# The last matrix product of a fused attention and two feed-forward layers: all twelve features by seven products, product number outermost

## The chip, the cores and the metric

The kernel runs on one core of one Trainium2 chip. The metric is the device time of one execution in microseconds (us). The engines are named as in the profile: PE (TensorE, matmuls), PEld (its weight loads), DVE (VectorE), ACT (ScalarE), POOL (GpSimd) and SP (SyncE, which issues the transfers).

## The reference, cut to what matters

```
def reference(...):                       # float32 in and out
    attn = causal attention of q, k, v    # 2 x 12 heads x 448 positions x 64
    x = attn.transpose(0, 2, 1, 3).reshape(896, 768)
    h = x @ w_in;  x = (h - tanh(h)) @ w_out          # 768 -> 2048 -> 768
    a = x @ w_a;   b = x @ w_b                        # 768 -> 1536 each
    return (a * b) @ w_o                              # 1536 -> 768
```

The change concerns the last line: the product of g = a * b (896 tokens, 1536 features) with w_o. In the kernel everything lies transposed: features on partitions in 12 blocks of 128 (f), tokens along the columns in two batches of 448 (B0, B1), outputs in 6 blocks of 128 (dm). The weights come as 64-bit floating point numbers, which the kernel makes into float32 on the chip.

## The kernel before, in words

**Precision.** Every float32 product is made of three matmuls of rounded operands: high by high, high by low and low by high (lines 275 to 284). So every operand, weight or feature, is made into two halves: ACT copies it into the high half, DVE subtracts that from the operand and writes the low half (`halve`, lines 600 to 602, for features; lines 244 and 253 for weights).

**Seven products.** Where two blocks of inputs, two of outputs and two batches stand together as 2 x 2 matrices, the kernel makes the four outputs with seven products in place of eight (a Strassen form after Winograd). The products have the numbers 1 to 7. Products 1 and 2 give one output, and 6, 3 and 5, 7, 4 are added up in the banks on the way to the others. The price is sums and differences of weights and of features, on DVE. One product over three blocks of inputs is 9 matmuls of 448 columns.

**Weights.** A weight tile (768 inputs by 128 outputs) is loaded in two transfers by SP's queue into one of three `raw` buffers (line 170), ACT casts its upper bits (line 179, `top`), DVE joins them with the lower ones to a float32 tile `t` (line 193, four buffers), and the halves `wh`, `wl` go into one of five pairs of buffers (WB). A list, `plan`, says in which order the weight halves are needed. `advance` (line 260) moves each of these steps one on, and every product calls it. `in_turn` (line 112) writes the plan of a stage in which the products of neighbouring outputs interleave.

**The stage of w_a and w_b.** Twelve units of two output blocks, w_a and w_b by turns, each by seven products over three pairs of inputs (`turn`, line 724): 63 matmuls a unit. `times` (line 710) multiplies the outcome of a w_b unit with that of the w_a unit before it, into the float32 features `g32`: one tile for each feature block, with both batches abreast.

**The last product.** Features 0 to 5 go by seven products with the pairs (0,3), (1,4), (2,5), and features 6 to 11 directly. For each of three pairs of outputs the kernel makes products 1, 5, 2, 3, 6, 7 and 4 (`seven`, 9 matmuls each), and between them four direct products of six features (`rest`, 18 matmuls each), which are added to the same banks. The terms of the features are made ahead: `early_terms` during the last unit of the stage before in the code, `late_terms` behind it. `kept` (line 856) copies a bank with ACT, `add` (line 696) adds a bank to a copy with DVE, `put` (line 861) issues the output's transfer.

**What sets the order.** The attention is written in an order by hand. After it, a scheduler places the instructions of each engine when the program is built, by its own estimates of their times; each engine then runs its list in that order, and waits where an instruction's inputs or buffers are not ready.

Of the kernel before, what the change touches and what calls it, by code (L numbers as in the profile page):

```python
# [9 lines left out]
F32 = mybir.dt.float32  # L10
F32R = mybir.dt.float32r
BF16 = mybir.dt.bfloat16
I32 = mybir.dt.int32
# [38 lines left out]
def attention_moe_moe2(ctx, tc, q, k, v, w_in, w_out, w_a, w_b, w_o, out):  # L52
# [22 lines left out]
    WB = 5  # L75
    scale = 1.0 / float(D) ** 0.5
# [62 lines left out]
    u0 = len(units)  # L139
    for f in range(0, NF2, 2):  # L140
        for w in (w_a, w_b):
            pair(w, f)
    in_turn(u0, True)
    for dm in range(0, KD, 2):
        pair(w_o, dm)
        u = len(units) - 1
        plan.extend((u, m) for m in (1, 5, 2, 3))
        whole(block(w_o, slice(DM, 2 * DM), dm))
        plan.extend((u, m) for m in (6, 7))
        whole(block(w_o, slice(DM, 2 * DM), dm + 1))  # L150
        plan.append((u, 4))
    last_use = {}
    for j, (i, m) in enumerate(plan):
        for x in (i,) if m is None else (units[i], units[i] + 1):
# [3 lines left out]
    thirds, summed = {}, set()  # L158
# [23 lines left out]
    def bits():  # L182

        i = at["bits"]
        while at["t"] in last_use and last_use[at["t"]] < at["halve"]:
# [6 lines left out]
        ts[i] = tp.tile([128, KD, 128], I32, tag="t", name="t")[:, 0:nk]  # L192
# [3 lines left out]
        at["bits"] += 1  # L196

    def source(j):

        i, m = plan[j]  # L200
        if m is None:
            return ts[i].bitcast(F32)
        if m == 7:
# [16 lines left out]

    def split_high():
# [4 lines left out]
        full = m is None  # L226
        if not full and j > at["halve"]:
            return
        if (i if full else units[i] + int(m not in (1, 2))) >= at["bits"]:
            return  # L230
# [6 lines left out]
        if m in (3, 5, 6, 7):  # L237
            combine(i, m)
# [471 lines left out]
    def times(u, q, x, on_chip):  # L710

        f, b = u // 2 * 2 + q // 2, q % 2
        if u % 2 == 0:
            if not on_chip:
                e = etile()
                nc.scalar.copy(out=e, in_=x)
                x = e
            left[q] = x
            return
        if f not in g32:  # L720
            g32[f] = g_full[0].tile([128, NT], F32, tag=("gwh", "gwl")[f // NK if f < KD else f % 2], name="g32")
        nc.vector.tensor_tensor(out=g32[f][:, BATCHES[b]], in0=x, in1=left.pop(q), op=ALU.mult)
# [72 lines left out]
    last, wide = [{} for _ in range(NK)], {}  # L795

    def early_terms(kk):

        g1, g2 = g32[kk], g32[kk + NK]
        t = [partp.tile([128, NT], F32R, tag="part", name="gpart") for _ in range(2)]  # L800
        last[kk][1], last[kk][5] = [[x[:, cs] for x in t] for cs in BATCHES]
        halve(*last[kk][1], g1[:, B0])
        minus(g1[:, B0], g1[:, B1], g1[:, B0])
        halve(*last[kk][5], g1[:, B0])
        minus(g1[:, B1], g2[:, B1], g1[:, B1])

    def roomy(f):

        if f == NF2 - 1:
            return small(2)  # L810
        pool, tags = (xp, ("xh", "xl")) if f < KD + NK else (xtra, ("th", "tl"))
        t = [pool.tile([128, NT], F32R, tag=x, name=x) for x in tags]
        return [[x[:, cs] for x in t] for cs in BATCHES]

    def split_wide(cs):

        for f in range(KD, NF2):
            if f not in wide:
                wide[f] = roomy(f)
            halve(*wide[f][cs.start // S], g32[f][:, cs])  # L820

    def late_terms():

        for kk in range(NK):
            t = [xp.tile([128, NT], F32R, tag=x, name=x) for x in ("xh", "xl")]
            last[kk][2], last[kk][3] = [[x[:, cs] for x in t] for cs in BATCHES]
        for m, cs in ((2, B0), (3, B1)):
            for kk in range(NK):
                halve(*last[kk][m], g32[kk + NK][:, cs])
        for kk in range(NK):  # L830
            g2 = g32[kk + NK]
            minus(g2[:, B1], g2[:, B1], g32[kk][:, B0])
            minus(g2[:, B0], g2[:, B0], g2[:, B1])
        split_wide(B0)
        for kk in range(NK):
            last[kk][7], = small()
            halve(*last[kk][7], g32[kk][:, B1])
        for m, cs in ((6, B1), (4, B0)):
            for kk in range(NK):
                t = g_full[0].tile([128, NT], F32R, tag="gwh", name="gwh")  # L840
                last[kk][m] = [t[:, x] for x in BATCHES]
                halve(*last[kk][m], g32[kk + NK][:, cs])
            if m == 6:
                split_wide(B1)

    def seven(o, m, go_on=False, done=1):

        wh, wl = next_weights()
        product(o, [((wh[:, kk], wl[:, kk]), last[kk][m]) for kk in range(NK)], go_on=go_on)
        at["done"] += done  # L850
        advance()

    def rest(w, o, cs, go_on=True):
        product(o, [((w[0][:, f - KD], w[1][:, f - KD]), wide[f][cs.start // S]) for f in wide], go_on=go_on)
# [14 lines left out]
    late_terms()  # L869
    for dm in range(0, KD, 2):  # L870
        o1, o5, o2, o3 = [next_bank()[:, :S] for _ in range(4)]
        seven(o1, 1)
        r0 = kept(o1)
        seven(o5, 5)
        r3 = kept(o5)
        seven(o2, 2)
        seven(o5, 3, True)
        w = next_weights()
        rest(w, o2, B0)
        add(r0, o2)  # L880
        put(dm, B0, r0)
        seven(o1, 6, True, 0)
        r1 = kept(o1)
        rest(w, o5, B1)
        add(r1, o5)
        put(dm, B1, r1)
        at["done"] += 3
        advance()
        seven(o1, 7, True)
        add(r3, o1)  # L890
        w = next_weights()
        rest(w, o3, B1, False)
        add(r3, o3)
        put(dm + 1, B1, r3)
        seven(o1, 4, True, 0)
        rest(w, o1, B0)
        put(dm + 1, B0, kept(o1))
        at["done"] += 4
        advance()
        advance()  # L900
# [27 lines left out]
```

## Time and profile before

| | us |
|---|---|
| runs | 558.43, 561.26, 558.07 |
| median | 558.43 |
| the profiled execution | 559.96 |
| its span | 558.2 |
| PE busy | 548.0 |
| DVE busy | 425.1 |
| ACT busy | 331.0 |

The profile shows one execution; its span begins with the first and ends with the last instruction, and 1.8 us of the execution's time lie around it. Busy times are of the whole span, which has stages with different limits: what a change in one stage is worth is read there. Matmuls are pipelined, so one that is busy for 0.37 us can start 0.2 us after the one before it.

### The profile page before, as it was taken

The numbers are of one execution on the slowest core, as the hardware profiler recorded it, in microseconds if no ns is written. First come the engines' busy times: TensorE is split into PE (matmuls) and PEld (weight loads), VectorE is DVE, ScalarE is ACT, GpSimd is POOL, SyncE is SP. The second block draws the span as 40 slices with busy tenths as digits, with TensorE's granted clock in tenths as the row PEclk, the third lists the DMA queues.
The fourth block names the chain that finished last, engine by engine and source line by source line (L and its number), as shares of the span: only waits on it lengthen the run. The fifth ranks groups of instructions, "written<-read, shape, count | busy, mean of one in ns | idle before, by whom it ended". The sixth has DMA issues, their size and how long they took to land.

```text
span 558.2 us, 8730 instructions
## 1 busy us (share of the span) xinstructions
PE 548.0 (98%) x3121; PEld 486.3 (87%) x3121; DVE 425.1 (76%) x876; ACT 331.0 (59%) x706; POOL 65.8 (12%) x88
## 2 busy tenths in 40 slices
PE   8999999998999999999999999999999999999997
PEld 4777788897999899899899889999999999999996
DVE  6897886479988867549879988979788699985311
ACT  6997996457677843238756464665554558754120
POOL 5688672200000000000000000000000000000000
PEclk9999999999999999999999999999999999999999
DMA  8825350067133742313741115335343533432001
GB/s 259 249 83 150 89 147 1 1 189 225 56 115 116 234 129 86 112 57 99 218 136 57 54 60 178 112 106 169 104 132 105 169 100 100 138 109 90 34 33 49
DMA packets 70827, 64.94 MB, mean 116 GB/s; under 512 B 13952, under 2 KB 70784, under 8 KB 70784
## 3 DMA queue, kind: packets, MB, share of 16 engines
q1 hardware_dynamic: 70784, 64.40, 37.0%
q8 instruction: 24, 0.39, 0.3%
q14 instruction: 19, 0.16, 0.1%
HBM read 61.63 MB, written 2.75 MB: 115 GB/s over the span
## 4 chain that ended last, share of the span: by engine, by line
PE 90%; DVE 3%; DMA 3%; ACT 2%; issue 1%; SPq 0%; DVEq 0%; ACTq 0%
PE s L280 37%; PE t L280 20%; PE h L280 13%; PE o L280 8%; PE o L432 4%; PE s L371 4%; PE t L406 3%; ACT p L392 1%; DMA raw<-in_moe_w_out 1%; PE t L451 1%; PE h L406 1%; DVE xsum L637 1%; DVE t L193 1%; DMA v<-in_v 1%; DMA raw<-in_moe_w_in 1%
## 5 line engine op out<-in xcount | busy, mean ns | idle before, releaser
L244 ACT CAST wh<-t 128x384 fp32r<-128x384 f32 (+2 forms) x154 | 81.9, 562 | 86.0 <-PE s L280 37.7
L179 ACT CAST top<-raw 128x768 f16<-128x768 bf16 (+1 forms) x70 | 73.8, 1054 | 44.7 <-DVE t L193 11.8
L253 DVE TENSOR_TENSOR wl<-t,wh 128x384 fp32r<-128x384 f32 (+2 forms) x149 | 87.0, 605 | 17.4 <-ACT wh L244 17.2
L193 DVE SCALAR_TENSOR_TENSOR t<-raw,top 128x768 int32<-128x768 int32 (+1 forms) x70 | 68.8, 985 | 4.0 <-ACT top L179 3.7
L280 PE MATMUL s<-xl,wh 128*128 128x448 f32 x150 | 55.0, 367 | 0.0
L280 PE MATMUL s<-xh,wl 128*128 128x448 f32 x150 | 54.7, 366 | 0.0
L280 PE MATMUL s<-xh,wh 128*128 128x448 f32 x150 | 54.2, 367 | 0.2 <-ACT e L733 0.2
L392 ACT ACTIVATE p<-p,m 112x448 f32<-112x448 f32 (+3 forms) x96 | 49.9, 524 | 5.6 <-DVE m L383 5.3
L697 DVE TENSOR_TENSOR e<-s,e 128x448 f32<-128x448 f32 x33 | 20.4, 620 | 31.8 <-PE s L280 31.5
L383 DVE CUSTOM_DVE_ANT_0 p<-s,mask 112x448 f32<-112x448 f32 (+3 forms) x96 | 37.9, 441 | 7.3 <-PE s L371 6.7
L280 PE MATMUL s<-gwl,wh 128*128 128x384 f32 (+2 forms) x96 | 34.9, 365 | 0.3 <-DVE gwl L558 0.3
L280 PE MATMUL s<-gwh,wl 128*128 128x384 f32 (+2 forms) x96 | 34.9, 365 | 0.0
L280 PE MATMUL s<-gwh,wh 128*128 128x512 f32 (+2 forms) x96 | 34.3, 364 | 0.0
L280 PEld LDWEIGHTS s<-xh,wh 128*128 128x128 f32 x150 | 28.2, 188 | 2.9 <-ACT e L733 0.6
L280 PEld LDWEIGHTS s<-xh,wl 128*128 128x128 f32 x150 | 28.2, 188 | 2.3
L280 PEld LDWEIGHTS s<-xl,wh 128*128 128x128 f32 x150 | 28.2, 188 | 2.3
L406 PE MATMUL t<-ident,p 112*112 112x112 f32 x195 | 27.6, 265 | 0.2 <-POOL qkh L351 0.2
L432 PE MATMUL o<-pt,v 112*64 112x224 f32 (+1 forms) x288 | 26.7, 326 | 0.9 <-DMA v<-in_v 0.9
L414 ACT COPY pt<-t 112x448 f32<-112x448 f32 (+1 forms) x39 | 18.4, 483 | 14.8 <-PE t L406 12.8
L432 PEld LDWEIGHTS o<-pt,v 112*64 112x64 f32 x288 | 19.1, 136 | 8.3 <-issue 1.1
L280 PE MATMUL h<-xh,wh 128*128 128x448 f32 x69 | 25.8, 374 | 0.0
L280 PE MATMUL h<-xh,wl 128*128 128x448 f32 x69 | 25.7, 372 | 0.0
(213 smaller groups left out, 1442.2 us busy)
## 6 DMA issues: line engine op xcount, KB each, us to landing
raw<-in_moe_w_out SPq DMA_DIRECT2D x48, 383.2 KB, 3.8
raw<-in_moe_w_in SPq DMA_DIRECT2D x32, 383.2 KB, 4.2
raw<-in_moe_w_a SPq DMA_DIRECT2D x24, 383.2 KB, 3.9
raw<-in_moe_w_b SPq DMA_DIRECT2D x24, 383.2 KB, 3.7
raw<-in_moe_w_out SPq DMA_DIRECT2D x12, 255.5 KB, 4.3
qk<-in_q SPq DMA_DIRECT2D x12, 224.0 KB, 3.3
qk<-in_k SPq DMA_DIRECT2D x12, 224.0 KB, 4.0
v<-in_v SPq DMA_DIRECT2D x24, 112.0 KB, 3.5
```

The source lines that it names most:

```text
L179: nc.scalar.copy(out=tops[i % len(tops)][:, 0:nk, :, 1], in_=top[:, :, :, 2])
L193: nc.vector.scalar_tensor_tensor(out=ts[i], in0=low[:, :, :, 0], scalar=13, in1=top, op0=ALU.logical_shift_right, op1=ALU.bitwise_or)
L244: nc.scalar.copy(out=halves[j][0], in_=x)
L253: engine.tensor_tensor(out=lo, in0=source(j), in1=hi.bitcast(F32), op=ALU.subtract)
L280: nc.tensor.matmul(o, a, b_, start=j == 0 and not go_on, stop=j == n - 1, skip_group_check=True)
L371: nc.tensor.matmul(sc[i, c][e], a[r, 0, cs], b_[r, 1, :n], start=x == 0, stop=x == len(terms) - 1)
L383: nc.vector.tensor_tensor_reduce(out=p[:, e], in0=s, in1=mask[:QC, S - n:], scale=-scale, scalar=3.0e38, op0=ALU.add, op1=ALU.min, accum_o ...
L392: nc.scalar.activation(out=p[:, e], in_=p[:, e], func=ACTF.Exp, bias=least[i][:, c, e:e + 1], scale=-1.0, accum_out=sums[i][:, c, e:e + 1],)
L406: nc.tensor.transpose(out=pst[:QC, x * QC:(x + 1) * QC], in_=blk, identity=ident[:QC, :QC])
L414: nc.scalar.copy(out=out_, in_=in_)
L432: nc.tensor.matmul(o[64 * e:64 * e + 64, cs], vt[:, k_, e, :], p.rearrange("s c q -> s (c q)"), start=k_ == 0, stop=k_ == 2 * h + 1, skip_ ...
L697: nc.vector.tensor_tensor(out=x, in0=o, in1=x, op=ALU.add)
```

## The change

All twelve features now go by the seven products: feature f is paired with f + 6, so that a product is 6 blocks of inputs, 18 matmuls. `g32` holds two neighbouring features of one batch abreast in a tile of 896 columns, so one instruction of ACT or DVE makes a term, or a half of it, for two features (`term`). The product number is outermost: product 1 for all three pairs of outputs, then 2, and so on in the order LAST; the outputs being added up stay in banks and copies meanwhile. The terms are made in the order of the products, a few ahead (AHEAD). A weight of the last product is a whole tile of 768 inputs, and its sums go over the whole tile (`combine_quad`). The six tiles of the odd output blocks (`of_last` with home "part") are loaded and joined between the tiles of w_a and w_b, from the sixth unit on; the other six keep their place behind them.

```diff
+    AHEAD = (1, 0, 2)
+    FIRST_LAST = 5
...
+    LAST = (1, 2, 5, 3, 6, 7, 4)
+    homes, quads = {}, {}
+    for n in range(KD // 2):
+        quads[u0 + NF2 + n] = {}
+
+    def of_last(n, r, f, home):
+        quads[u0 + NF2 + n][1 + r, 1 + f] = len(tiles)
+        homes[len(tiles)] = home
+        tiles.append(block(w_o, slice(f * DM, (f + 1) * DM), 2 * n + r))
+
     for f in range(0, NF2, 2):
         for w in (w_a, w_b):
             pair(w, f)
+            n = len(units) - 1 - u0 - FIRST_LAST
+            if 0 <= n < KD:
+                of_last(n // 2, 1, n % 2, "part")
     in_turn(u0, True)
-    for dm in range(0, KD, 2):
-        pair(w_o, dm)
-        u = len(units) - 1
-        plan.extend((u, m) for m in (1, 5, 2, 3))
-        whole(block(w_o, slice(DM, 2 * DM), dm))
-        plan.extend((u, m) for m in (6, 7))
-        whole(block(w_o, slice(DM, 2 * DM), dm + 1))
-        plan.append((u, 4))
+    for f in range(2):
+        for n in range(KD // 2):
+            of_last(n, 0, f, "t" if 3 * f + n < 4 else ("th", "tl")[n % 2])
+    units.extend([None] * len(quads))
+    plan.extend((u, m) for m in LAST for u in quads)
...
-        if i >= at["abs"] or i >= at["t"] + TP:
+        home = homes.get(i, "t")
+        held_ = sum(homes.get(x, "t") == "t" for x in range(at["t"], i))
+        if i >= at["abs"] or home == "t" and held_ >= TP or home in ("th", "tl") and not last_turned:
...
+        if home == "t":
+            ts[i] = tp.tile([128, KD, 128], I32, tag="t", name="t")[:, 0:nk]
+        else:
+            t = (partp if home == "part" else xtra).tile([128, NT], I32, tag=home, name="tlast")
+            ts[i] = t[:, 0:KD * 128].rearrange("p (k n) -> p k n", n=128)
...
+        if home == "part" and i in [x[2, 2] for x in quads.values()]:
+            a21, a22 = [ts[i_].bitcast(F32) for x in quads.values() if x.get((2, 2)) == i for i_ in (x[2, 1], i)]
+            nc.vector.tensor_tensor(out=a21, in0=a21, in1=a22, op=ALU.add)
...
+    WHERE = {1: (1, 1), 2: (1, 2), 5: (2, 1), 3: (1, 2), 6: (1, 1), 7: (1, 1), 4: (2, 2)}
...
+    def combine_quad(u, m):
+
+        def less(o, a, b_):
+            nc.vector.tensor_tensor(out=o, in0=a, in1=b_, op=ALU.subtract)
+
+        if m == 3:
+            less(quad(u, 1, 1), quad(u, 2, 1), quad(u, 1, 1))
+            less(quad(u, 1, 2), quad(u, 1, 2), quad(u, 1, 1))
+        elif m == 7:
+            less(quad(u, 1, 1), quad(u, 2, 2), quad(u, 1, 1))
...
-        if f not in g32:
-            g32[f] = g_full[0].tile([128, NT], F32, tag=("gwh", "gwl")[f // NK if f < KD else f % 2], name="g32")
-        nc.vector.tensor_tensor(out=g32[f][:, BATCHES[b]], in0=x, in1=left.pop(q), op=ALU.mult)
+        p = u // 2, b
+        if p not in g32:
+            g32[p] = g_full[0].tile([128, NT], F32, tag=("gwh", "gwl")[b], name="g32")
+        nc.vector.tensor_tensor(out=g32[p][:, BATCHES[f % 2]], in0=x, in1=left.pop(q), op=ALU.mult)
...
-    def early_terms(kk):
...
-    def late_terms():
...
+    NP = NF2 // 4
+    last, terms_at = {}, [0]
+
+    def term():
+
+        n = terms_at[0]
+        if n >= len(LAST) * NP:
+            return
+        terms_at[0] += 1
+        m, p = LAST[n // NP], n % NP
+        b11, b12, b21, b22 = g32[p, 0], g32[p, 1], g32.get((p + NP, 0)), g32.get((p + NP, 1))
+        x = {1: b11, 2: b21, 5: b11, 3: b22, 6: b11, 7: b12, 4: b21}[m]
+        if m == 5:
+            minus(b11, b12, b11)
+        elif m == 6:
+            minus(b11, b22, b11)
+        elif m == 7:
+            minus(b12, b22, b12)
+        elif m == 4:
+            minus(b21, b21, b11)
+        pool, tags = (xp, ("xh", "xl")) if n % 7 < 6 else (xtra, ("th", "tl"))
+        t = [pool.tile([128, NT], F32R, tag=x, name="last") for x in tags]
+        halve(*t, x)
+        last[m, p] = t
+
+    def all_of(u, m, o, go_on=False):
 
         wh, wl = next_weights()
+        parts = [((wh[:, k], wl[:, k]), [x[:, BATCHES[k % 2]] for x in last[m, k // 2]]) for k in range(KD)]
+        product(o, parts, go_on=go_on)
+        at["done"] += 2
 
...
-        if u - u0 == NF2 - 1 and m in (2, 5, 6):
-            early_terms({2: 0, 5: 1, 6: 2}[m])
...
+        if u - u0 == NF2 - 1 and m == 3:
+            for _ in range(NP):
+                term()
+    last_turned.append(True)
+    term()
+    acc = {}
+    for m in LAST:
+        for n, u in enumerate(quads):
+            if m in (1, 2, 5):
+                acc[n, m] = bank({1: "sss", 2: "tto", 5: "sht"}[m][n])[:, :S]
+            o = acc[n, {6: 1, 7: 1, 4: 1, 3: 5}.get(m, m)]
+            all_of(u, m, o, m in (3, 6, 7, 4))
+            if m == 1:
+                c1[n] = kept(o)
+            elif m == 2:
+                add(c1[n], o)
+                put(2 * n, B0, c1[n])
+            elif m == 5:
+                z[n] = kept(o)
+            elif m == 6:
+                c2[n] = kept(o)
+                add(c2[n], acc[n, 5])
+                put(2 * n, B1, c2[n])
+            elif m == 7:
+                add(z[n], o)
+                put(2 * n + 1, B1, z[n])
+            elif m == 4:
+                put(2 * n + 1, B0, kept(o))
+            for _ in range(AHEAD[n]):
+                term()
+            advance()
```

Three places in the order of the instructions show the move. The first is SP's queue in the stage of w_a and w_b (`in_moe_w_out` is w_o here, x4 means four equal transfers). Before, all of w_o stands behind it:

```order
L170 DMA raw<-in_moe_w_b 128x3x511 x4
L170 DMA raw<-in_moe_w_a 128x3x511 x4
L170 DMA raw<-in_moe_w_b 128x3x511 x4
L170 DMA raw<-in_moe_w_out 128x3x511 x22
L862 DMA out<-e 128x448 x3
L170 DMA raw<-in_moe_w_out 128x3x511 x2
```

Now:

```order
L182 DMA raw<-in_moe_w_a 128x3x511 x4
L182 DMA raw<-in_moe_w_out 128x3x511 x2
L182 DMA raw<-in_moe_w_b 128x3x511 x4
L182 DMA raw<-in_moe_w_out 128x3x511 x2
L182 DMA raw<-in_moe_w_a 128x3x511 x4
L182 DMA raw<-in_moe_w_out 128x3x511 x2
L182 DMA raw<-in_moe_w_b 128x3x511 x4
L182 DMA raw<-in_moe_w_out 128x3x511 x12
```

Two transfers of w_o, one tile, stand between those of w_a and w_b, six times in all, of which the last three are shown; the other six tiles follow in one row, and no output goes out ahead of a load any more.

The second place is DVE in the passage to the last product, around the last features of a batch to be made (`g32_...<-s_...`, line 722 before, 768 now; numbers tell buffers apart). Before:

```order
L193 SCALAR_TENSOR_TENSOR t_5310<-raw_5001,top0_83 128x768
L602 TENSOR_TENSOR tl_5189<-g32_5057,th_5188 128x448
L218 TENSOR_TENSOR t_5287<-t_5287 128x384
L602 TENSOR_TENSOR gwh_5213<-g32_4347,gwh_5213 128x448
L722 TENSOR_TENSOR g32_5130<-s_5004,e_5032 128x448
L253 TENSOR_TENSOR wl_5303<-t_5268,wh_5302 128x384
L193 SCALAR_TENSOR_TENSOR t_5347<-raw_5270,top1_84 128x768
L219 TENSOR_TENSOR t_5268<-t_5287,t_5268 128x384
L602 TENSOR_TENSOR gwh_5216<-g32_4391,gwh_5216 128x448
L253 TENSOR_TENSOR wl_5303<-t_5287,wh_5302 128x384
L602 TENSOR_TENSOR gl_5193<-g32_5130,gh_5192 128x448
```

Now:

```order
L768 TENSOR_TENSOR g32_5118<-e_5091,e_5000 128x448
L298 TENSOR_TENSOR wl_5276<-tlast_4102,wh_5275 128x768
L650 TENSOR_TENSOR g32_3880<-g32_4657,g32_3880 128x896
L252 TENSOR_TENSOR tlast_5186<-tlast_5186,t_4939 128x768
L768 TENSOR_TENSOR g32_5079<-s_5040,e_5062 128x448
L252 TENSOR_TENSOR tlast_5213<-tlast_5213,t_5018 128x768
L298 TENSOR_TENSOR wl_5301<-tlast_4349,wh_5300 128x768
L650 TENSOR_TENSOR g32_4410<-g32_5118,g32_4410 128x896
L650 TENSOR_TENSOR g32_4612<-g32_4612,g32_3880 128x896
L647 TENSOR_TENSOR last_5237<-g32_5079,last_5236 128x896
```

The features are followed by sums and halves of whole weight tiles (lines 252 and 298), two differences for later terms (line 650) and then the low half of their own term (`last_5237`, line 647), the last pair's for product 2; before, the halves were of one feature and one batch.

The third place is PE where that term is first used (line 325; `t_5249`, `t_5279` and `o_5304` are the banks of product 2, `s_5338` and `h_5369` those of product 5; `last_5236` is the high half, `last_5237` the low one):

```order
L325 MATMUL s_5338<-last_5241,wl_5276 128x448
L325 MATMUL t_5249<-last_5236,wh_5120 128x448
L325 MATMUL t_5279<-last_5236,wh_5209 128x448
L325 MATMUL o_5304<-last_5236,wh_5245 128x448
L325 MATMUL h_5369<-last_5241,wl_5301 128x448
L325 MATMUL h_5369<-last_5241,wh_5300 128x448
L325 MATMUL h_5369<-last_5242,wh_5300 128x448
L325 MATMUL h_5369<-last_5241,wl_5301 128x448
L325 MATMUL s_5338<-last_5271,wh_5275 128x448
L325 MATMUL h_5369<-last_5271,wh_5300 128x448
L325 MATMUL t_5249<-last_5237,wh_5120 128x448
```

Product 2 is broken off before its last pair, and product 5 is begun for two output blocks ahead of it; the first matmul that needs the low half is the last row. Between the end of the last product of the unit before the last (bank `t_4990`) and this row stand 168 matmuls. The order before breaks products off too, at terms of single features.

## Rows read from the trace of the kernel before

**Rows 1.** Page section 1: busy time, share of the span, instructions; section 2: granted clock by 40 slices.

```profile
PE 548.0 (98%) x3121; PEld 486.3 (87%) x3121; DVE 425.1 (76%) x876; ACT 331.0 (59%) x706; POOL 65.8 (12%) x88
...
PEclk9999999999999999999999999999999999999999
```

**Rows 2.** Page section 4: share of the span of the chain that ended last.

```profile
PE 90%; DVE 3%; DMA 3%; ACT 2%; issue 1%; SPq 0%; DVEq 0%; ACTq 0%
```

**Rows 3.** Windows: busy us (instructions) of each engine, granted clock, DMA share, GB/s.

```profile
440.00:460.00 20.00, 20.00 (x100) 18.54 (x99) 15.10 (x27) 11.40 (x21) 0.00 (x0) 1.00 0.30 98
460.00:480.00 20.00, 20.00 (x101) 18.53 (x100) 19.49 (x36) 16.95 (x33) 0.00 (x0) 1.00 0.44 139
480.00:500.00 20.00, 20.00 (x100) 18.28 (x99) 17.49 (x32) 11.16 (x21) 0.00 (x0) 1.00 0.28 91
500.00:520.00 20.00, 20.00 (x98) 18.17 (x97) 11.63 (x20) 7.20 (x12) 0.00 (x0) 1.00 0.28 96
520.00:540.00 20.00, 20.00 (x98) 18.17 (x97) 5.29 (x8) 4.31 (x8) 0.00 (x0) 1.00 0.10 37
```

**Rows 4.** Chain in order of time: start us, length us, engine, bank, line, matmuls.

```profile
451.50 3.65 PE s L280 x18
...
525.33 5.58 PE t L280 x27
```

**Rows 5.** Timeline: start us, length us, instruction [idle before, released by], PE's one wait.

```profile
498.55 0.36 PE L280 MATMUL s<-gh,wl 128*128 128x448 f32 x1
...
498.82 0.30 PEld L280 LDWEIGHTS t<-gwh,wh 128*128 128x128 f32 x2 [0.28 <-DVE e L697]
```

**Rows 6.** Timeline of the end.

```profile
554.52 0.37 PE L280 MATMUL t<-gh,wl 128*128 128x448 f32 x1
554.92 0.53 ACT L858 COPY e<-t 128x448 f32<-128x448 f32 x1 [13.93 <-PE t L280]
555.48 0.33 SPq L862 DMA_DIRECT2D out<-e  x1
```

**Rows 7.** Timeline of DVE: a wait for PE, and steps of 448, 384 and 768 columns.

```profile
459.03 0.62 DVE L697 TENSOR_TENSOR e<-t,e 128x448 f32<-128x448 f32 x1 [0.24 <-PE t L280]
...
469.35 0.62 DVE L605 TENSOR_TENSOR g<-g,g 128x448 f32<-128x448 f32 x1
469.89 0.62 DVE L605 TENSOR_TENSOR g<-g 128x448 f32<-128x448 f32 x1
470.42 0.55 DVE L253 TENSOR_TENSOR wl<-t,wh 128x384 fp32r<-128x384 f32 x1
470.89 0.95 DVE L193 SCALAR_TENSOR_TENSOR t<-raw,top 128x768 int32<-128x768 int32 x1
471.76 0.55 DVE L253 TENSOR_TENSOR wl<-t,wh 128x384 fp32r<-128x384 f32 x1
```

**Rows 8.** Timeline of ACT: a wait for a load, and steps of 384, 448, 768 columns.

```profile
437.27 1.08 ACT L179 CAST top<-raw 128x768 f16<-128x768 bf16 x1 [1.98 <-DMA raw<-in_moe_w_out]
...
462.26 1.08 ACT L179 CAST top<-raw 128x768 f16<-128x768 bf16 x1
463.20 1.03 ACT L601 CAST xh<-g 128x448 fp32r<-128x448 f32 x2
464.13 0.51 ACT L244 CAST wh<-t 128x384 fp32r<-128x384 f32 x1
464.54 1.03 ACT L601 CAST xh<-g 128x448 fp32r<-128x448 f32 x2
465.48 0.84 ACT L244 CAST wh<-t 128x768 fp32r<-128x768 f32 x1
466.22 0.52 ACT L716 COPY e<-h 128x448 f32<-128x448 f32 x1
```

**Rows 9.** Waits from 380 to 460 us: us in total, times, longest.

```profile
DVE e L697 <- PE s L280: 12.3, 6, 2.5
```

**Rows 10.** Page section 6: transfers of w_out and w_o, KB each, us to landing.

```profile
raw<-in_moe_w_out SPq DMA_DIRECT2D x48, 383.2 KB, 3.8
```

More of the change, by code (lines that the diff above doesn't have):

```diff
@@ L142, in attention_moe_moe2 @@
             pair(w, f)
+            n = len(units) - 1 - u0 - FIRST_LAST
+            if 0 <= n < KD:
+                of_last(n // 2, 1, n % 2, "part")
     in_turn(u0, True)
-    for dm in range(0, KD, 2):
-        pair(w_o, dm)
-        u = len(units) - 1
-        plan.extend((u, m) for m in (1, 5, 2, 3))
-        whole(block(w_o, slice(DM, 2 * DM), dm))
-        plan.extend((u, m) for m in (6, 7))
-        whole(block(w_o, slice(DM, 2 * DM), dm + 1))
-        plan.append((u, 4))
+    for f in range(2):
[3 more added lines that the diff above has]
+    plan.extend((u, m) for m in LAST for u in quads)
     last_use = {}
     for j, (i, m) in enumerate(plan):
-        for x in (i,) if m is None else (units[i], units[i] + 1):
+        for x in () if i in quads and m else (i,) if m is None else (units[i], units[i] + 1):
             last_use[x] = j
@@ L157, in attention_moe_moe2 @@
     at = {"load": 0, "abs": 0, "bits": 0, "high": 0, "halve": 0, "use": 0, "done": 0, "t": 0, "slots": 0}
-    thirds, summed = {}, set()
+    thirds, summed, last_turned = {}, set(), []
     def load_part():
@@ L184, in bits @@
         i = at["bits"]
-        while at["t"] in last_use and last_use[at["t"]] < at["halve"]:
+        while at["t"] in homes and homes[at["t"]] != "t" or last_use.get(at["t"], at["halve"]) < at["halve"]:
             at["t"] += 1
-        if i >= at["abs"] or i >= at["t"] + TP:
+        home = homes.get(i, "t")
+        held_ = sum(homes.get(x, "t") == "t" for x in range(at["t"], i))
+        if i >= at["abs"] or home == "t" and held_ >= TP or home in ("th", "tl") and not last_turned:
             return
@@ L202, in source @@
             return ts[i].bitcast(F32)
+        if i in quads:
+            return quad(i, *WHERE[m])
         if m == 7:
@@ L225, in split_high @@
         i, m = plan[j]
-        full = m is None
-        if not full and j > at["halve"]:
+        full = m is None or i in quads
+        if m is not None and j > at["halve"]:
             return
-        if (i if full else units[i] + int(m not in (1, 2))) >= at["bits"]:
+        if i in quads and m is not None:
+            need = quads[i][1, 1 if m == 1 else 2]
+        else:
+            need = i if full else units[i] + int(m not in (1, 2))
+        if need >= at["bits"]:
             return
@@ L236, in split_high @@
             at["pair"] = [w_p.tile([128, KD, 128], F32R, tag=x, name=x) for x in ("wh", "wl")]
-        if m in (3, 5, 6, 7):
+        if m is not None and i in quads:
+            combine_quad(i, m)
+        elif m in (3, 5, 6, 7):
             combine(i, m)
@@ L793, in attention_moe_moe2 @@
                 pass
-    last, wide = [{} for _ in range(NK)], {}
-    def early_terms(kk):
[L799 to L820, printed above, removed]
-    def late_terms():
[L824 to L844, printed above, removed]
@@ L846, in seven @@
-    def seven(o, m, go_on=False, done=1):
-        wh, wl = next_weights()
[L849 to L854, printed above, removed]
+    NP = NF2 // 4
[20 more added lines that the diff above has]
+        last[m, p] = t
@@ L865, in attention_moe_moe2 @@
     for u, m in stages[-1]:
-        if u - u0 == NF2 - 1 and m in (2, 5, 6):
-            early_terms({2: 0, 5: 1, 6: 2}[m])
         turn(u, m, lambda u, q, x, on_chip: times(u - u0, q, x, on_chip))
[L869 to L900, printed above, removed]
+        if u - u0 == NF2 - 1 and m == 3:
[29 more added lines that the diff above has]
+            advance()
 _INS = ["q", "k", "v"]
```

3 lines of the change are left out of this document (2 added, 1 removed).

## Prediction

> **What bounds the kernel now.** I began with the busy times. TensorE (PE) is busy 548.0 of 558.2 us [rows 1], and its granted clock stands at the full level throughout (1.00, the 2.4 GHz level). The chain that ended last says the same: 90% of it is PE, and no other engine has more than 3% [rows 2]. In windows of 20 us PE is busy without a break from 440 to 540 us [rows 3], across the passage into the last product. VectorE (DVE) is nearly full there, 19.49 and 17.49 of 20 us, and then empties to 11.63 and 5.29. So the stage that changes is bound by the number of its matmuls, and the work of the other engines costs something only where it makes PE wait.
>
> The price of a matmul comes from runs in the chain [rows 4]. Eighteen matmuls of 448 columns take 3.65 us, 202.8 ns each; from about 499 us on 27 take 5.58 us, 206.7 ns each. The step rises at one place: PE waits 0.28 us for a VectorE addition at 498.8 us [rows 5], and runs at 206.7 ns from there to the end, with the same granted clock. After the last matmul come a ScalarE copy and one output transfer [rows 6]; the change ends with the same two.
>
> **What is removed.** An output pair took 7 x 9 matmuls for six features and 4 x 18 for the others, 135; three pairs, 405. Now it is 3 pairs x 7 products x 18 = 378. That is 27 fewer, each with its weight load, which PE runs beside the matmul before it. In the stretch where the old ones ran: 27 x 206.7 ns = **5.58 us**, all on the path, since PE does not pause [rows 3]. The Trainium skill, "TensorE: Matmul & The Clock Gate", section "Wait — 56ns, not 53.3ns?", gives the start-to-start time as columns by 2.4 GHz and some 2.5 ns, 189 ns for 448 columns; by that the term would be an estimated 5.1 us. These rows show 203 and 207 ns, so they decide.
>
> **The step of the rest.** From 498.8 us on the old kernel ran 271 matmuls at the longer step (56.0 us / 206.7 ns). The 244 that remain of them save 3.9 ns each, 1.0 us, if the longer step does not come; if it comes as before, nothing. I know only that it began at a wait. I take half, 0.5 us. The wait of 0.28 us itself goes, since the instruction that it stood before is gone; whether another replaces it is the next question.
>
> **What is added to VectorE and ScalarE.** The unit for both is start to start: on VectorE 0.47 us for 384 columns, 0.535 for 448, 0.87 for 768 [rows 7]; on ScalarE 0.41, 0.47 and 0.74, and 0.94 for the cast that opens a weight tile [rows 8]. No row has 896 columns. It is bounded by 0.87 (768 columns) and 1.07 (two of 448) on VectorE; the line through 384 and 768 gives 1.00, which I take. ScalarE likewise: between 0.74 and 0.94, I take 0.85.
> - Weights of the last product: 21 halves of 384 columns and 6 of 768 become 21 of 768. VectorE +3.2 us, ScalarE +2.5.
> - Weight sums: 12 of 384 become 12 of 768, VectorE +4.8.
> - Feature terms: 33 halves and 12 differences of 448 become 21 and 12 of 896: VectorE 24.1 to 33.0, +8.9; ScalarE 15.5 to 17.9, +2.4.
> - Bank additions: 12 become 9, VectorE -1.6.
>
> VectorE gains some 15 us of work, 65 in all beside 378 x 203 ns = 77 us of PE; the old kernel left it idle for 23 us between 500 and 540 [rows 3]. On the average it fits, with some 11 us to spare.
>
> **What is moved.** Six of the twelve output weight tiles (12 loads on SP's queue, 6 casts on ScalarE, 6 joins and 3 sums on VectorE) go between those of w_a and w_b. VectorE there: 9 x 0.87 = 7.8 us more; the early feature terms, 12 x 0.535 = 6.4, leave: +1.4 over six units of 63 matmuls, 76 us, in which VectorE is some three quarters busy and waits for PE (12.3 us in 80 for bank s alone) [rows 3, 9]. ScalarE +6 x 0.94 - 6 x 0.47 = +2.8. For loads a tile comes each 76/18 = 4.2 us instead of 6.4; with three raw buffers and 3.8 us to land [rows 10] that is enough, though ScalarE has already waited 1.98 us for a load in this stage [rows 8]. I cost it at nothing; its cover is that PE has up to ten products of weights ahead, and without it the price is bounded by 1.4 + 2.8 = 4.2 us.
>
> **The tight place.** It is the passage into the last product. The last pair's second term needs the features that the last unit makes. On VectorE 38 instructions stand from the first whole weight tile of the new stage (wl_5035) to the low half of that term (last_5237): 16 of 768 columns, 15 of 896, 7 of 448; 16 x 0.87 + 15 x 1.00 + 7 x 0.535 = 32.7 us. The first comes after a bank addition that waits for PE (such additions waited 0.24 us for PE in the old kernel too [rows 7]: VectorE is not behind there) and after ScalarE's 0.74 us of the same tile, so about 1.0 us after that product's end. The list ends at 33.8 us. Until it needs the term, PE has 168 matmuls of work, some of it put ahead out of turn: 168 x 202.8 ns = 34.1 us. So it just holds. With the bounds for 896 columns the list ends between 31.8 and 34.8 us: a wait of 0 to 0.7 us. ScalarE's cast of a raw tile stands in the same passage ahead of the first terms; each microsecond by which its load is late moves the list by up to 1. I take **0.4 us** of wait, range 0 to 1. Behind the term the same count leaves 0.8 us at one weight tile (wl_5335), then 3 us and growing.
>
> **Sum.** 5.58 + 0.28 + 0.5 - 0.4 = 6.0 us less. The profiled execution took 559.96 us, its span 558.2; the changed one is to take 554.0 with a span of 552.2. The median of the runs, 558.43 (558.07 to 561.26), is 1.53 below that execution; from it the change gives **552.4 us**, 1.1% less.
>
> **Rivals.**
> 1. *VectorE is late and PE waits.* If an instruction that depends on the one before starts only when that has ended, the list costs durations: 0.95 for 768 columns and 0.62 for 448 [rows 7], on the same line 1.08 for 896: 35.7 us, ending at 36.8, a wait of 2.7 us where I put 0.4. The same size comes of a load that is 2 to 3 us late. For it: this margin is the smallest of the change. Against it: rows of 448 and 768 columns start 0.08 us before their predecessor ends, over whole runs. It gives 552.4 + 2.3 = 554.7, and 553.6 to 556.6 with the bounds. The Trainium skill, "VectorE: DVE Perf Modes", section "The DRAIN you can't avoid", states that the next instruction does not start until the pipe is empty, which would make this the rule; it adds that one that no wait holds starts earlier. The starts above speak for the second, but most of the new list depends on what stands shortly ahead. Chance 0.22.
> 2. *The gain comes back.* The early tiles hold up w_a and w_b by their bound of 4.2 us, and the passage costs 1 to 3. 558.4 - 6.4 + 4.2 + 2 = 558.2, from 556.6 to 561. Against it: the old kernel ran a like load in the same windows with one wait of 0.28 us [rows 5]. Chance 0.09.
> 3. *Slower.* The terms share seven buffers, 21 terms in turn, and a term's buffer comes free only when the product of seven terms before has used it in all three output blocks. If each product's terms came only as that product begins, ScalarE's half, VectorE's difference and VectorE's half (0.95, the 0.84 of 768 columns [rows 8] by its step's line, + 1.08 + 1.08, 3.1 us) would stand open before each of the six later products: 18.7 us, 558.4 - 6.4 + 18.7 = 570.7. It decides from the point at which a buffer is released less than one product (3.7 us) before it is needed. Against it: seven buffers are more than two products' three, so there are 11 us, one whole product, between. Chance 0.05.
>
> That the matmuls do not become fewer can be left out: the order of the changed program has 378 of them.
>
> **Chances and range.** My forecast (PE bound, waits up to 1 us in all, either step) has 0.62 and 551.4 to 553.6 us; the remaining 0.02 lies below it. The range, 551.0 to 556.6 us, takes in the forecast and the first rival and leaves out about 0.15. About 1%, 5.6 us, is what a measurement can tell from no change; that is 552.8 us. Some three quarters of the forecast and what lies below it end under that mark: faster 0.49. Within 1%: the rest of the forecast, the first rival and most of the second, 0.46. Slower by over 1%: 0.05.
>
> **What would show it.** Right: 27 matmuls fewer, PE without a break from 440 us to the last one, VectorE busy to within 20 us of the end. Wait for the term: an idle time of PE, with VectorE's low half (line 647) named, some 34 us after the last unit but one. Rival 2: PE idle before that, with weights (lines 289 or 298) named. Rival 3: such waits at each of six places some 11 us apart. The step: runs of 18 matmuls at 3.65 or at 3.72 us near the end. The prediction is wrong if PE waits more than 1 us in all for terms or weights, or if matmuls slow down elsewhere.

## The result, and the profile after

| | before | after |
|---|---|---|
| median (range), us | 558.42 (558.07 to 561.26) | 552.79 (552.15 to 554.2) |
| ratio | | 0.9892 [0.9853, 0.9931] |
| the profiled execution, us | 559.96 | 552.17 |

The forecast was 552.4 us, from 551.0 to 556.6.

The page of the changed kernel, busy times, granted clock and the shares of the chain, against [rows 1, 2]:

```profile
PE 541.7 (98%) x3094; PEld 481.4 (87%) x3094; DVE 440.5 (80%) x855; ACT 335.0 (61%) x688; POOL 65.8 (12%) x88
...
PEclk9999999999999999999999999999999999999999
...
PE 88%; DVE 4%; ACT 3%; DMA 3%; issue 1%; SPq 0%; POOL 0%; DVEq 0%; ACTq 0%
```

PE has 27 matmuls fewer, DVE 15.4 us of work more. The same windows as [rows 3] (PE, PEld, DVE, ACT, POOL, granted clock, DMA):

```profile
440.00:460.00 20.00, 20.00 (x100) 18.55 (x99) 14.44 (x25) 10.08 (x18) 0.00 (x0) 1.00 0.39 122
460.00:480.00 20.00, 20.00 (x101) 18.53 (x100) 19.67 (x23) 12.53 (x17) 0.00 (x0) 1.00 0.00 1
480.00:500.00 20.00, 20.00 (x100) 18.33 (x99) 20.00 (x24) 12.13 (x16) 0.00 (x0) 1.00 0.03 12
500.00:520.00 20.00, 20.00 (x101) 18.53 (x100) 20.00 (x24) 12.06 (x16) 0.00 (x0) 1.00 0.07 24
520.00:540.00 20.00, 20.00 (x100) 18.54 (x99) 9.20 (x13) 4.48 (x7) 0.00 (x0) 1.00 0.19 70
```

PE is still full; DVE, which emptied from 500 us on in the old kernel, now is full from 480 to 520 us as well. The passage itself, in the timeline: DVE's bank addition behind which the list begins, the start of the list, two neighbours of 896 columns' work, and the place where list and PE meet; then the end, against [rows 6]:

```profile
458.02 0.62 DVE L742 TENSOR_TENSOR e<-t,e 128x448 f32<-128x448 f32 x1 [1.18 <-PE t L325]
458.69 0.96 DVE L298 TENSOR_TENSOR wl<-t,wh 128x768 fp32r<-128x768 f32 x1
...
463.92 1.08 DVE L650 TENSOR_TENSOR g<-g,g 128x896 f32<-128x896 f32 x1
464.92 0.95 DVE L298 TENSOR_TENSOR wl<-t,wh 128x768 fp32r<-128x768 f32 x1
...
490.77 4.09 DVE L647 TENSOR_TENSOR last<-g,last 128x896 fp32r<-128x896 f32 x4
...
491.66 0.36 PE L325 MATMUL h<-last,wh 128*128 128x448 f32 x1
491.91 0.47 PE L325 MATMUL t<-last,wh 128*128 128x448 f32 x1
492.22 0.36 PE L325 MATMUL t<-last,wl 128*128 128x448 f32 x1
...
491.91 0.19 PEld L325 LDWEIGHTS t<-last,wh 128*128 128x128 f32 x1 [0.26 <-DVE last L647]
...
546.73 0.37 PE L325 MATMUL s<-last,wl 128*128 128x448 f32 x1
547.13 0.53 ACT L875 COPY e<-s 128x448 f32<-128x448 f32 x1 [3.12 <-PE s L325]
```

The first of the four low halves at 490.77 is last_5237; it ends some 1.08 us later, at 491.85, and PE's weight load for it starts at 491.91, 33.9 us after the product that ended at 457.98 (first row of the next fence). The load waited 0.26 us, but the matmul itself came 0.25 us after the one before it, and the next one 0.31 us after that, where 0.20 is usual: the path lost 0.15 us. The chain of PE to the end, against [rows 4]:

```profile
456.15 1.83 PE t L325 x9
...
499.67 3.65 PE t L325 x18
...
514.46 32.65 PE s L325 x161
```

Eighteen matmuls take 3.65 us, 202.8 ns each, to the last one: the longer step of [rows 4] did not come.

### The profile page after: what moved, and what is told of

It reads as the page before. It is cut to its first block, busy times and chain, and to the rows that moved or that the text cites. A ratio compares the mean times of both kernels' runs of the same rounds, so it can differ in the third digit from the quotient of the medians.

```text
span 550.4 us, 8625 instructions
## 1 busy us (share of the span) xinstructions
PE 541.7 (98%) x3094; PEld 481.4 (87%) x3094; DVE 440.5 (80%) x855; ACT 335.0 (61%) x688; POOL 65.8 (12%) x88
## 4 chain that ended last, share of the span: by engine, by line
PE 88%; DVE 4%; ACT 3%; DMA 3%; issue 1%; SPq 0%; POOL 0%; DVEq 0%; ACTq 0%
PE s L325 41%; PE t L325 17%; PE h L325 13%; PE o L325 7%; PE o L477 4%; PE s L416 3%; PE t L451 3%; ACT p L437 2%; DVE t L211 1%; DMA raw<-in_moe_w_out 1%; DVE xsum L682 1%; PE t L496 1%; DMA v<-in_v 1%; DMA raw<-in_moe_w_in 1%; ACT pt L459 1%
## 5 line engine op out<-in xcount | busy, mean ns | idle before, releaser
L191 ACT CAST top<-raw 128x768 f16<-128x768 bf16 (+1 forms) x70 | 73.9, 1055 | 49.3 <-DVE t L211 13.4
L298 DVE TENSOR_TENSOR wl<-t,wh 128x384 fp32r<-128x384 f32 (+2 forms) x136 | 81.7, 624 | 6.7 <-ACT wh L289 6.5
L211 DVE SCALAR_TENSOR_TENSOR t<-raw,top 128x768 int32<-128x768 int32 (+1 forms) x62 | 61.1, 988 | 2.1 <-ACT top L191 1.7
L325 PE MATMUL s<-last,wh 128*128 128x448 f32 x168 | 48.0, 365 | 0.0
L325 PE MATMUL s<-xl,wh 128*128 128x448 f32 x123 | 45.1, 367 | 0.0
L325 PE MATMUL s<-xh,wl 128*128 128x448 f32 x123 | 44.8, 365 | 0.0
L325 PE MATMUL s<-xh,wh 128*128 128x448 f32 x123 | 44.4, 367 | 0.2 <-ACT e L779 0.2
L325 PEld LDWEIGHTS s<-last,wh 128*128 128x128 f32 x168 | 31.6, 188 | 2.5
L325 PE MATMUL s<-last,wl 128*128 128x448 f32 x84 | 30.5, 365 | 0.0
L398 POOL TENSOR_TENSOR qkl<-qk,qkh 128x448 fp32r<-128x448 f32 x22 | 25.1, 1146 | 1.0
L325 PEld LDWEIGHTS s<-xh,wh 128*128 128x128 f32 x123 | 23.1, 188 | 2.4 <-ACT e L779 0.6
```

The source lines that it names most:

```text
L191: nc.scalar.copy(out=tops[i % len(tops)][:, 0:nk, :, 1], in_=top[:, :, :, 2])
L211: nc.vector.scalar_tensor_tensor(out=ts[i], in0=low[:, :, :, 0], scalar=13, in1=top, op0=ALU.logical_shift_right, op1=ALU.bitwise_or)
L298: engine.tensor_tensor(out=lo, in0=source(j), in1=hi.bitcast(F32), op=ALU.subtract)
L325: nc.tensor.matmul(o, a, b_, start=j == 0 and not go_on, stop=j == n - 1, skip_group_check=True)
L398: nc.gpsimd.tensor_tensor(out=lo[:, x], in0=qk[i][:, x], in1=hi[:, x].bitcast(F32), op=ALU.subtract)
```

## A common start for the comparisons

Executions of one kernel differ by 1 us and more ahead of the change. So the traces below are compared from one event, the start of the bank addition above (line 742, 697 before), to the end of the last matmul:

| kernel | addition | last matmul ends | between | matmuls behind the product that it reads | from the 2601st matmul to the end |
|---|---|---|---|---|---|
| before | 459.03 | 554.89 | 95.9 | 467 | 107.0 |
| before, another execution | 457.76 | 552.55 | 94.8 | 467 | 105.9 |
| after | 458.02 | 547.10 | 89.1 | 439 | 100.4 |
| after, again | 457.33 | 546.50 | 89.2 | 439 | 100.5 |

The fifth column is the number of matmuls in the trace. It falls by 28 and not by 27: in the new order one more matmul stands ahead of the event, so 0.2 us of the difference in "between" belongs to the event and not to the change. The last column counts by matmuls alone, from the start of the 2601st to the end of the last; it has exactly 27 fewer in the new kernel.

Between the profiled executions this stretch shrank by 6.6 us; the other 1.2 us of 7.8 lay ahead of it and are no part of the change. The six early tiles are loaded ahead of it too, and cost nothing there: from the 1701st to the 2601st matmul the two executions of before take 183.0 and 183.2 us, those of after 183.0 and 183.1.

## Experiments

Each run was timed beside the kernel before, and ratios are to it. It took 558.7 us beside light and less_early_light, 560.3 beside less_early_none, and 558.2 to 558.5 beside the others. "More than after", said of a median, is against the second timing of the changed kernel, 551.75 us. "From the 2601st matmul" is the stretch of the last column above; after takes 100.4 us for it.

**Before and after once more.** Nothing edited.

> The changed kernel once more, in the same company as the kernels beside it. If the matmul step of the rest (202.8 or 206.7 ns) belongs to the program, it is 202.8 ns to the end again, and the time is 552.2 to 552.8 us. If it comes by chance at a wait, some executions have the longer step from somewhere in the last product on, up to 1.0 us more.

Measured: 551.75 us (551.41 to 552.07), ratio 0.9873 [0.985, 0.9897], step 202.8 ns to the end, the same wait at line 647.

> The kernel before once more, for a second profile. If the wait of 0.28 us and the step of 206.7 ns behind it belong to its order, both show again near 498 us; if by chance, the matmuls run at 202.8 ns to the end and the execution is 1.0 to 1.3 us shorter than the first profiled one. The wait of 1.1 us for a partial sum near 127 us, which only the first profile had, is expected to be gone.

Measured: 557.62 us, one execution. The chain of PE in this execution of the old kernel, where [rows 5] had the wait and [rows 4] the longer step:

```profile
497.65 5.66 PE t L280 x27
503.30 3.65 PE o L280 x18
...
547.08 5.49 PE t L280 x27
```

The same wait stands in the first run (it takes 0.18 us more than 27 x 202.8 ns = 5.48), but the step is 202.8 ns behind it, and 203.3 in the last run. So the longer step belonged to the first execution, not to the wait. From this execution to that of after the stretch from the 2601st matmul shrank by 105.9 - 100.4 = 5.5 us: 27 x 202.8 ns = 5.48, and 0.03 because the old wait cost the path 0.18 us and the new one 0.15.

**The early weights behind the others.**

```diff
-            n = len(units) - 1 - u0 - FIRST_LAST
-            if 0 <= n < KD:
-                of_last(n // 2, 1, n % 2, "part")
...
+    for n in range(KD):
+        of_last(n // 2, 1, n % 2, "part")
...
-            need = quads[i][1, 1 if m == 1 else 2]
+            need = quads[i][{1: (1, 1), 2: (1, 2)}.get(m, (2, 2))]
```

> The six tiles of the odd output blocks are loaded and joined behind the other six, not between those of w_a and w_b. Theory (VectorE's list is the limit of the passage, the early conversion pays for it): nine instructions of 0.87 us and their casts stand in the passage; counted along VectorE's list the halves of product 5 come 8.5 to 11.5 us after PE could use them, so 9 to 12 us more than the changed kernel, 562 to 565 us, and idle time of PE named with weight halves or casts. Rival (the conversion is hidden wherever it stands): within 1 us of the changed kernel.

Measured: 565.96 us (564.15 to 567.17), ratio 1.0124 [1.0094, 1.0153], 14.2 more than after and 1.0 above what was expected; from the 2601st matmul it is 113.8, 13.4 more. PE's three longest waits from 440 us on (us in total, times, longest), and two windows:

```profile
PEld s L324 <- DVE wl L297: 6.5, 1, 6.5
PEld t L324 <- DVE last L646: 1.8, 1, 1.8
PEld h L324 <- ACT wh L288: 1.4, 1, 1.4
```

```profile
500.00:505.00 5.00, 1.41 (x4) 1.28 (x5) 5.00 (x7) 0.00 (x0) 0.00 (x0) 0.50 0.13 48
505.00:510.00 5.00, 5.00 (x16) 4.42 (x15) 5.00 (x7) 0.08 (x1) 0.00 (x0) 0.53 0.25 92
```

The waits are those expected, on DVE and on its weights (lines are one less in this kernel). What the expectation lacked is the clock: after these waits it is granted at 0.50, the 1.2 GHz level, and a full window holds 16 matmuls where 26 fit. So the place of the six tiles, which the sum held at nothing, is what makes the change a gain: late, it is slower than before.

**The early loads five units sooner: FIRST_LAST 5 becomes 0.**

> The six early tiles go between those of w_a and w_b from the first unit on, not from the sixth. Theory (VectorE and ScalarE have room in the whole stage, the price of the early conversion is zero): within 0.5 us of the changed kernel. Rival (the room is small and was chosen): PE waits in the first units, named with weight halves, 1 to 4 us more.

Measured: 553.42 us (553.0 to 554.45), ratio 0.9906 [0.9886, 0.9926], 1.7 more than after (0.6 more than after's first median). The rival came true and not the theory. PE waits in the first units of w_a and w_b, between 322 and 351 us, for high halves of weights and features above all:

```profile
PEld s L325 <- ACT wh L289: 1.0, 2, 0.8
PEld s L325 <- ACT xh L646: 0.7, 1, 0.7
```

From the 1701st to the 2601st matmul it takes 184.6 us, where before and after take 183.0 to 183.2. At line 647 PE then loses only 0.07 us, and the step is the longer one from there on:

```profile
501.02 3.72 PE t L325 x18
...
516.10 33.29 PE s L325 x161
```

From the 2601st matmul it is 101.4 us, 1.0 more than after: some 270 matmuls x 3.9 ns are 1.05. So the place of the loads among the units does cost: nothing from the sixth unit on, some 1.4 us from the first.

**Halves for each feature alone.**

```diff
+    def each(f, *xs):
+        for cs in BATCHES:
+            f(*[x[:, cs] for x in xs])
...
-        halve(*t, x)
+        each(halve, *t, x)
```

and the differences of products 5, 6, 7 and 4 in the same way.

> Each term is made in two halves of 448 columns with two instructions each, and each difference likewise, in place of one of 896. Theory (the passage is bound by start-to-start steps on VectorE, with no margin): 33 pairs cost 0.07 us each more, 2.3 us in all, and counted along the list the second half of the term of the last pair comes 2.1 to 2.4 us late: 2 to 3 us more than the changed kernel, 554.5 to 555.5 us. Rival (there is still room beside PE): no difference beyond 0.5 us. A gain would mean that the wider instructions delay their readers.

Measured: 557.14 us (555.45 to 558.24), ratio 0.9969 [0.9953, 0.9986], 5.4 more than after, where 2 to 3 were expected. PE's waits:

```profile
PEld s L325 <- DVE g L768: 1.6, 1, 1.6
PEld t L325 <- DVE last L647: 1.1, 1, 1.1
PEld t L325 <- DVE e L742: 1.1, 1, 1.1
```

There are three places, not one: a bank that DVE reads late (line 768), the term, and a bank addition. PE stood idle 2.7 us in them; by the starts of its matmuls it lost 3.5, and the step behind the second of them is 206.7 ns. From the 2601st matmul it is 104.7 us, 4.3 more than after. So 896 columns in one instruction are a condition of most of the gain too.

**27 matmuls fewer late, or early.** Both leave out 27 products of low weight by high feature; the diff is the late one, the early one has the cuts {1: 4, 2: 5}.

```diff
-        product(o, parts, go_on=go_on)
+        cut = {7: 4, 4: 5}.get(m, 0)
+        n = 18 - cut
+        j = 0
+        for k, ((ah, al), (bh, bl)) in enumerate(parts):
+            for a, b_ in ((ah, bh), (ah, bl), (al, bh))[:2 if k < cut else 3]:
+                nc.tensor.matmul(o, a, b_, start=j == 0 and not go_on, stop=j == n - 1, skip_group_check=True)
+                j += 1
```

> 27 matmuls (low weight by high feature) are left out of products 7 and 4, behind the tight place. Theory (PE alone sets the time there, VectorE has room): 27 x 203 ns = 5.5 us less than the changed kernel, 546 to 547 us, no new wait. Rival (VectorE's list is the limit of the whole last product): PE waits for it and less than half of the 5.5 us is gained.

Measured: 546.65 us (546.21 to 548.71), ratio 0.9789 [0.9767, 0.9812]; from the 2601st matmul it is 95.1, 5.3 less than after. Behind the passage matmuls are the bound and pay in full; 0.14 us of their 5.48 is lost at the wait for the term, which costs 0.29 us in this execution.

> 27 matmuls (low weight by high feature) are left out of products 1 and 2, in front of the tight place; VectorE's list stays. Theory: PE gains 27 x 202 ns = 5.5 us and then waits 4.7 to 5.4 us for the same list (last term of product 2, weight of product 5), so the time stays within 1 us of the changed kernel. Rival (PE alone sets the time of the last product): 5.5 us less, 547 us.

Measured: 555.02 us (552.27 to 556.16), ratio 0.9923 [0.9891, 0.9955]: 3.3 slower than after, with 27 matmuls fewer. It missed what was expected, which was within 1 us. The five executions differ by 3.9 us, and the traced one is the slowest of them. PE's two longest waits in the timeline, and its windows:

```profile
486.60 0.68 PE L875 MATMUL h<-last,wh 128*128 128x448 f32 x2 [0.72 <-ACT wh L289]
489.78 1.11 PE L875 MATMUL s<-last,wh 128*128 128x448 f32 x2 [2.51 <-DVE g L768]
```

```profile
485.00:490.00 5.00, 1.78 (x8) 0.99 (x7) 5.00 (x8) 1.07 (x2) 0.00 (x0) 0.86 0.00 0
490.00:495.00 5.00, 5.00 (x14) 4.44 (x15) 5.00 (x6) 4.91 (x6) 0.00 (x0) 0.50 0.00 0
```

PE gets to the end of its work sooner and waits there, longest for DVE. It is granted half the clock afterwards: 14 matmuls instead of 26 in a window, which is 12 x 202.8 ns = 2.4 us. The step behind it is 206.7 ns, 1.0 us more. The expectation had the waits, but neither the clock nor the step. From the 2601st matmul it is 102.5 us, 2.1 more than after.

**A lighter DVE ahead of the term.** Products 5 and 6 take their features without the differences, which leaves out six instructions of 1.00 us.

```diff
-        if m == 5:
-            minus(b11, b12, b11)
-        elif m == 6:
-            minus(b11, b22, b11)
-        elif m == 7:
+        if m == 7:
```

> Left out: the six differences on VectorE (896 columns, 1.00 us each) that products 5 and 6 need, so VectorE's work ahead of the tight term is up to 6 us shorter and TensorE's is the same. Theory: the list delays TensorE by no more than the 0.26 us seen at the low half (line 647), so the time stays within 0.5 us of the changed kernel's (551.4 to 552.8), and the wait at line 647 is gone. Rival: VectorE's list holds TensorE up by more than the waits show; then it gets 1 us or more faster (550.8 or less).

Measured: 552.99 us (552.94 to 554.55), ratio 0.9896 [0.9863, 0.9929], 0.2 outside what was expected. PE does not wait in the passage any more, and from the 2601st matmul it is 100.3 us, 0.1 less than after, which is the 0.15 that after lost at line 647. So DVE held PE up by no more than the waits show.

> Left out: the same six differences, and the 27 matmuls (low weight by high feature) of products 1 and 2 whose removal alone gave 555.0 us, with waits of 2.9, 1.1 and 0.4 us. Theory: those waits came from VectorE's list alone; with 6 us of it gone the 27 matmuls pay their 5.5 us and the clock stays at 1.00: 546.3 to 547.5 us. Rival: the waits come from something else in that stretch (ScalarE's high halves, the transfers): then 551 us or more, and TensorE waits there for ScalarE.

Measured: 550.84 us (550.16 to 552.32), ratio 0.9856 [0.9816, 0.9897]. Missed: PE still waits 0.72 and 1.67 us and the clock falls to 0.72 in the window from 485. DVE and PE:

```profile
469.77 1.09 DVE L647 TENSOR_TENSOR last<-g,last 128x896 fp32r<-128x896 f32 x1 [1.65 <-ACT last L646]
...
474.05 1.08 DVE L650 TENSOR_TENSOR g<-g,g 128x896 f32<-128x896 f32 x1
...
478.86 1.09 DVE L650 TENSOR_TENSOR g<-g,g 128x896 f32<-128x896 f32 x1
...
484.73 1.09 DVE L650 TENSOR_TENSOR g<-g,g 128x896 f32<-128x896 f32 x1
485.74 0.62 DVE L768 TENSOR_TENSOR g<-s,e 128x448 f32<-128x448 f32 x1
...
486.41 0.67 PE L871 MATMUL s<-last,wh 128*128 128x448 f32 x2 [1.67 <-DVE g L768]
```

Part of the time that came free went into a wait of DVE for ScalarE's high half (1.65 us), and three differences of product 7 stand behind that wait, ahead of the read of the bank (line 768) that PE waits for.

**All differences left out.** Those of products 7 and 4 as well.

> Left out: all differences of the features (products 5, 6, 7 and 4), and the 27 matmuls of products 1 and 2. With the differences of products 5 and 6 alone left out, TensorE still waited 1.67 us for VectorE's read of a PSUM tile (line 768), and in VectorE's order three differences of product 7 (1.00 us each) still stood between its last wait for ScalarE and that read. Theory: VectorE's order up to that read sets the wait, so the read comes 3 us sooner, the wait goes, the clock stays at 1.00, and the time is 546.3 to 548.3 us (0.7 us of it for a wait for the high half of a weight tile). Rival: the wait is set by something else, ScalarE or TensorE's own tiles: 550 us or more and the wait at line 768 stays above 1 us.

Measured: 547.11 us (546.0 to 548.61), ratio 0.977 [0.9723, 0.9818]. The read comes 13.0 us after DVE's wait for ScalarE, where it came 16.0 after, PE waits nowhere in the passage, and the clock stays at 1.00:

```profile
470.59 1.09 DVE L647 TENSOR_TENSOR last<-g,last 128x896 fp32r<-128x896 f32 x1 [1.64 <-ACT last L646]
...
483.56 0.61 DVE L768 TENSOR_TENSOR g<-s,e 128x448 f32<-128x448 f32 x1
```

From the 2601st matmul it is 94.8 us, 5.6 less than after. So the 27 matmuls pay here too, once DVE's order up to that read is 3 us shorter. It was DVE that held less_early up. The shorter wait, for ScalarE's high half of a weight, went with it, though the expectation had left 0.7 us for it.

**Differences of products 6 and 7 on GpSimd.**

```diff
-            minus(b11, b22, b11)
+            nc.gpsimd.tensor_tensor(out=b11, in0=b22, in1=b11, op=ALU.subtract)
...
-            minus(b12, b22, b12)
+            nc.gpsimd.tensor_tensor(out=b12, in0=b22, in1=b12, op=ALU.subtract)
```

> The six differences of features for products 6 and 7 are made by GpSimd, which has nothing to do in this part; four of them stand in VectorE's list ahead of the tight term. Theory: the list is 4 us shorter, the last wait of PE goes, nothing else moves: 0 to 0.4 us less than the changed kernel (551.4 to 551.8 us), and no execution shows the longer matmul step. Rival (GpSimd holds VectorE up while both work in the same memory): VectorE's steps get longer than 1.00 us for 896 columns, PE waits, and the time is 1 us or more above it.

Measured: 560.53 us (559.12 to 562.0), ratio 1.0036 [1.002, 1.0052], 8.8 more than after: missed. GpSimd, DVE and PE in the timeline:

```profile
466.37 2.55 POOL L858 TENSOR_TENSOR g<-g,g 128x896 f32<-128x896 f32 x1 [361.10 <-ACT wh L289]
470.03 2.83 POOL L858 TENSOR_TENSOR g<-g,g 128x896 f32<-128x896 f32 x1 [1.12 <-DVE g L650]
470.79 2.89 DVE L298 TENSOR_TENSOR wl<-t,wh 128x768 fp32r<-128x768 f32 x1
...
483.17 7.32 POOL L856 TENSOR_TENSOR g<-g,g 128x896 f32<-128x896 f32 x1 [10.31 <-DVE last L647]
487.56 0.95 DVE L252 TENSOR_TENSOR tlast<-tlast,t 128x768 f32<-128x768 f32 x1
490.53 2.95 DVE L650 TENSOR_TENSOR g<-g,g 128x896 f32<-128x896 f32 x1 [2.02 <-POOL g L856]
...
494.94 1.00 PE L325 MATMUL s<-last,wh 128*128 128x448 f32 x2 [3.90 <-DVE g L768]
```

DVE and GpSimd do not work beside each other here. A half of 768 columns, 0.95 us elsewhere, takes 2.89 while GpSimd subtracts; and GpSimd's third subtraction, begun while DVE runs seven instructions without a gap, ends only 2.0 us after the last of them, 7.32 us in all. The half ends 0.82 us after the subtraction beside it (473.68 and 472.86 us), about its own usual length. The Trainium skill, "SBUF — State Buffer", section "SBUF: two separate sides", says that the two share a pair of ports which one instruction holds to its end, also where DVE has two inputs in SBUF and GpSimd reads there too; the trace agrees, with 2.89 us for 0.95 on DVE and 7.32 us on GpSimd, whose other five took 2.1 to 3.0. The expectation counted GpSimd as a free hand, and DVE's queue stood behind it.

## Why the prediction was right, step by step

- **27 matmuls, 5.58 us.** Right: 5.48 at 202.8 ns, shown between two executions of equal step, where 5.5 went, and by less_late, which took 27 more away for 5.3 us.
- **The step, 0.5 us.** A number between two cases. Between the two profiled executions it brought the full 1.0 us; between the second one of before and after, nothing. It belongs to the execution: that it "began at a wait" misled, since the same wait left it alone in the second. Half of it was a guess, and that the sum lies between the two cases is in part luck.
- **The old wait, 0.28 us.** It is gone, and PE had lost 0.18 us by it.
- **The wait for the term, 0.4 us, range 0 to 1.** Right in place and kind, too large in size; the path lost 0.15. Together with the old wait that is 0.03 us gained, where the sum had 0.12 lost. DVE's list took from 458.69 to 491.85, 33.2 us, where 32.7 were worked out, and began 0.7 us after the product's end, not 1.0. 896 columns step by 1.00 us (463.92 to 464.92), the value taken. ScalarE's high half held the list up for 0.33 us.
- **15 us more on DVE, hidden.** Measured 15.4, and light shows that the path would be shorter by no more than 0.1 us without 6 of them. The "11 us to spare" were an average: in the passage the margin is nil, as less_early and halves_448 show.
- **The early weights, nothing.** Right for the place that was chosen: 183.0 to 183.2 us from the 1701st to the 2601st matmul in both kernels. Not every place is free: from the first unit on (early0) the same stretch takes some 1.4 us more, inside the bound of 4.2. Without the early loading the passage itself pays 13.4 (late_weights), a price that the bound did not look at.
- **Rival 1** fell on DVE's starts: the next instruction begins 0.08 us before its predecessor's record ends, in the whole list, but for its one wait. **Rivals 2 and 3**: from 440 us on PE waits nowhere but at the term, neither for weights nor at later products.
- **The sum.** 6.0 us were to go; 5.6 went between the medians, 5.5 from the 2601st matmul on in two executions of equal step, and 6.6 in the two of unequal step. That the median came within 0.4 us of the forecast is in part luck: the four times of the old kernel alone lie 3.2 us apart. No run takes back by itself the order with the product number outermost, so its own share stays open.

## What to carry to other kernels

Removing matmuls pays their full time only where PE is the bound on the spot: the same 27 were worth 5.3 us behind the tight place, and cost 2.1 ahead of it (from the 2601st matmul). Count the list of the other engine up to the instruction that PE needs, in starts, and check which waits in that list would use up what you take out of it. Compare executions from an event just ahead of the change; their earlier parts differ by as much as a small gain. Count that the same work stands behind the event in both: here one matmul more or less looked like 0.2 us of a wait. And look at the part ahead of the event too, where a move can cost something, as in early0.

## What the runs showed of the hardware

- Waits of PE can cost more than themselves. In less_early 3.2 us of idle time between 485 and 490 us were followed by a granted clock of 0.50, and cost 2.4 us more; in less_early_light 2.4 us in two places were followed by 0.72 in a window of 5 us, in sums_pool 3.9 us in one place by 0.66. In halves_448 2.7 us in three places between 491 and 505 us left it at 1.00.
- The step of a matmul of 448 columns is 202.8 or 206.7 ns at a granted clock of 1.00. The longer one came behind a wait of PE in before, early0, halves_448, late_weights and less_early and stayed to the end, and did not come behind like or longer waits in before's second execution, after, less_early_light and sums_pool. What decides it stays open.
- GpSimd took 2.1 to 3.0 us for a difference of 896 columns that DVE makes in steps of 1.00, and 7.32 us for the one begun in a run of DVE without gaps (sums_pool). Five instructions of DVE with two inputs in SBUF that began beside one of the others took 2.9 to 3.0 us in place of 0.95 to 1.09.
